# First sequence's k, q and v loaded in runs of six tokens and turned head by head, with the ranks of the first parts drawn anew

## The chip, the cores and the metric

The kernel runs on one core of a Trainium2 chip. The metric is the time of one execution on the device in microseconds (us), and the number given for a kernel is the median of several runs. PE is the engine of matrix products, DVE the vector engine, ACT the scalar engine, POOL and SP two more; SP's queue issues nearly all transfers. Each engine takes its instructions strictly in the order in which the program has them.

## What is computed

The inputs are q, k, v (8 sequences, 8 heads, 576 tokens, 64 numbers each), 32 packed queries p per head, two mixing vectors and three weight matrices. The weights come as 64-bit floats.

```python
def sm_attn(qq, kk, vv):                       # per head
    s = scale * qq @ kk.T;  a = softmax(s);  return a @ vv
x  = sm_attn(q, pp, pp)  with  pp = sm_attn(p, k, v)      # heads side by side: 8 x 576 x 512
xk = mu_k * x + (1 - mu_k) * x_prev;  xr = mu_r * x + (1 - mu_r) * x_prev   # x_prev: the token before
out = sigmoid(xr @ w_r) * (relu(xk @ w_k) ** 2 @ w_v)
```

## The kernel before

The 4608 tokens are worked off in nine blocks of 512. Every block needs products with w_r (the gates), w_k (the keys) and w_v (the values), and each of these is done three times in a reduced format with a high and a low part (`wr_h`, `wr_l`, `xh`, `xl`), so that one chunk of one tile is a triple of products 128x512. These triples are most of PE's work. The attention of a sequence is squeezed between them.

A planner inside the program (`Flow`) sets the order of everything. Each piece of work is a generator that says which engine it wants for how long by the planner's own estimate; the planner takes the piece that can start first, and ranks (the numbers `FIRST`, `RANK_...`, `RANK_LATE...`) break ties. The order is written into the program when it is built and nothing of it is decided on the chip. While the first sequence is under way, the planner puts products of the identity with itself into a spare bank (`fill`, L1809) wherever it believes PE to be idle. They are instructions like others: PE carries them out whether it has time or not.

The first sequence has a path of its own, in two halves h of four heads (two pairs each):

- `first_pair` loads a pair of heads of k or q into a tile `raw` of 96 partitions: token 96 c + p lies on partition p, so every piece moved is one token of one head, 256 bytes. There is one transfer per head.
- `transposed_on_pe` (k) and `first_transposed` (q, in two halves) turn a pair with six products per pair in transpose mode, 128 columns wide (L467, L498), and DVE and ACT copy the result from PSUM into `kT` and `qT`.
- `first_side(h)` is the chain: scores of p with k (`s1`, L560), the maximum (L793), the exponential (L800), the turning of the weights (L814, L815), their copy `aT` (L831 on ACT for h = 0, L826 on DVE for h = 1), the sum over v (`pv`, L581), the scaled result `pm` and its turning (`pT`, L602), the scores of q (`s2`, L615), a softmax over 32 columns (L628 to L641), the turning back (L648), its copies `a2t` (L653, L655), and the mixed inputs by products with the shares (`mixed_on_pe`, L969), whose high part ACT writes (L980) and whose low part DVE writes (L982).
- `first_gates` then does the gates of block 0 (L1128 to L1130). It begins when chunk 0 of half 0 is there and needs chunks 2 and 3 from half 1.
- `convert` splits a piece of a weight matrix into its two parts: three steps on ACT (L334, L336, L348) and two on DVE (L339, L350), from the transfer `st` on. There are 4 pieces of w_r, 8 of w_k and 8 of w_v.

Eight semaphores serve the transfers of SP and ACT in turn, so that a transfer waits for the one eight places before it. PSUM has two double banks `pa` for the large results of attention and single banks `m`.

Of the kernel before, what the change touches and what calls it, by code (L numbers as in the profile page):

```python
# [182 lines left out]
def attn_pack_channel_mix(ctx: ExitStack, tc: tile.TileContext, q, k, v, p, mu_k, mu_r, w_k, w_v, w_r, out):  # L183
# [4 lines left out]
    P = 128  # L188
# [17 lines left out]
    FIRST = 12.453, 12.081, 16.585, 10.332  # L206
    RANK_1, RANK_MIX, RANK_KEYS, RANK_R, RANK_W, RANK_W2, RANK_V, LOADS_1, RANK_SQ, RANK_REST, HOLD_V, HOLD_S = 14.383, 2.279, 9.364, 21.382, 11.434, 11.544, 16.223, 19.391, 0.152, -6.533, 0.05, 0.25
    RANK_LATE1 = -1.021
    RANK_LATE2 = 7.09
    RANK_LATE3 = 9.434  # L210
    RANK_LATE4 = 10.248
    RANK_LATE5 = 2.56
    RANK_LATE6 = 9.599
    RANK_LATE7 = 3.494
    RANK_LATE8 = 20.327
    RANK_LATE9 = 10.578
    RANK_LATE10 = 7.095
    RANK_LATE11 = 3.446
    RANK_LATE13 = 29.829
    RANK_LATE14 = 4.595  # L220
    RANK_LATE12 = 8.964
# [64 lines left out]
    for tag, n, size in (  # L286
        ("xk", NC, 2 * TB), ("sq", NF, 2 * TB), ("tmp", 4, WP), ("sig", 4, DM), ("kq", 4, S), 
        ("raw", 3, S), ("a2", 1, S), ("ex", 7, TB), ("e", 2, S), ("aT", 1, 5 * P), ("vt", 2, NPR * 5 * D),
# [3 lines left out]
    for j, size in enumerate((S, 5 * P)):  # L292
        sb.tile([P, size], F32, name="a", tag=f"a{j}")
# [94 lines left out]
    def loads(b):  # L388
        flow.spawn(packed(b), lrank(b) - 0.03)
        for src, tag in ((k, "kT"), (v, "vt"), (q, "qT")):  # L390
# [5 lines left out]
            for pr in range(NPR):  # L396
# [3 lines left out]
                if b < EARLY:  # L400

                    raw = tile_([P, 6, 2 * D], F32, space, slot, "raw")
                    for hh in range(2):
                        yield from load(
                            raw[:T6, :, hh * D:(hh + 1) * D], src[b, 2 * pr + hh].rearrange("(c p) d -> p c d", p=T6),
                            0.51, 0.6,
                        )
                        back_to_issue()
                    flow.spawn(transposed_on_pe(tag, b, pr, space, slot, raw), rank(b), flow.free["dma"] + LANDS)
                    continue  # L410

# [14 lines left out]
    def values_of(b, h):  # L426
# [4 lines left out]
        if b < MOVED:  # L431
# [25 lines left out]
    def transposed_on_pe(tag, b, pr, raw_space, raw_slot, raw):  # L457
# [6 lines left out]
        yield pe(0.66)  # L464
# [1373 lines left out]
```

## Time and profile before

| what | us |
|---|---|
| median of 3 runs (575.17 to 576.54) | 575.51 |
| the profiled execution's own time | 575.83 |
| its span in the trace | 574.0 |
| PE busy in the span (98%) | 564.7 |
| first product of the gates begins at | 31.94 |
| first product of the keys of block 0 begins at | 52.76 |

The span runs from the first instruction to the last; 1.83 us of the profiled execution lie outside it. A product's row in the trace is longer than the time after which the next one starts (390 ns on average against starts 0.23 us apart for the 128x512 products), so that the starts, not the durations, show the pace. One product of ordinary 32-bit numbers leaves two rows in the trace, one in transpose mode or in the reduced format leaves one. A filler leaves two.

### The profile page before, as it was taken

The numbers are of one execution on the slowest core, as the hardware profiler recorded it, in microseconds if no ns is written. First come the engines' busy times: TensorE is split into PE (matmuls) and PEld (weight loads), VectorE is DVE, ScalarE is ACT, GpSimd is POOL, SyncE is SP. The second block draws the span as 40 slices with busy tenths as digits, with TensorE's granted clock in tenths as the row PEclk, the third lists the DMA queues.
The fourth block names the chain that finished last, engine by engine and source line by source line (L and its number), as shares of the span: only waits on it lengthen the run. The fifth ranks groups of instructions, "written<-read, shape, count | busy, mean of one in ns | idle before, by whom it ended". The sixth has DMA issues, their size and how long they took to land.

```text
span 574.0 us, 9929 instructions
## 1 busy us (share of the span) xinstructions
PE 564.7 (98%) x3702; PEld 443.4 (77%) x3702; DVE 426.5 (74%) x792; ACT 342.0 (60%) x607; POOL 7.3 (1%) x36
## 2 busy tenths in 40 slices
PE   8999999999999999999999999999999999999996
PEld 7867767787677777777868777877788888888885
DVE  3797799928698778656982798078676799687974
ACT  2689979436376594374743585357545767645910
POOL 4000000000000000000000000000000000000000
PEclk9999999999999999999999999999999999999999
DMA  9898766664674660863466373200010010000025
GB/s 215 267 265 252 172 153 126 158 124 100 121 180 85 120 145 3 207 132 71 104 139 139 48 147 107 71 1 0 16 59 1 1 74 0 1 0 2 0 51 97
DMA packets 188000, 56.76 MB, mean 99 GB/s; under 512 B 165288, under 2 KB 180144, under 8 KB 187952
## 3 DMA queue, kind: packets, MB, share of 16 engines
q1 hardware_dynamic: 183536, 55.21, 41.8%
q10 hardware_dynamic: 4160, 0.66, 0.6%
q8 instruction: 29, 0.48, 0.4%
q0 software_dynamic: 256, 0.26, 0.2%
q14 instruction: 19, 0.16, 0.1%
HBM read 43.13 MB, written 12.98 MB: 98 GB/s over the span
## 4 chain that ended last, share of the span: by engine, by line
PE 78%; DVE 9%; ACT 6%; DMA 4%; SPq 2%; issue 1%; POOL 0%; ACTq 0%; DVEq 0%; POOLq 0%
PE ph L1083 8%; PE ph L1084 8%; PE ph L1085 8%; PE pvo L1179 7%; PE ph L1363 7%; PE pvo L1180 7%; PE pvo L1181 6%; PE ph L1640 6%; PE pr L1150 4%; PE pr L1151 4%; PE pr L1152 4%; DVE x L1050 3%; DMA st<-in_moe_w_r 2%; PE pa L923 2%; SPq L242 2%
## 5 line engine op out<-in xcount | busy, mean ns | idle before, releaser
L1179 PE MATMUL pvo<-wv_h,sq 128*128 128x512 f32 x224 | 89.3, 399 | 0.8 <-ACT r L1095 0.8
L1083 PE MATMUL ph<-xk,wk_h 128*128 128x512 f32 x224 | 89.5, 399 | 0.0
L1084 PE MATMUL ph<-xk,wk_h 128*128 128x512 f32 x224 | 87.4, 390 | 0.0
L1180 PE MATMUL pvo<-wv_l,sq 128*128 128x512 f32 x224 | 87.4, 390 | 0.0
L1085 PE MATMUL ph<-xk,wk_l 128*128 128x512 f32 x224 | 87.3, 390 | 0.0
L1181 PE MATMUL pvo<-wv_h,sq 128*128 128x512 f32 x224 | 87.3, 390 | 0.0
L1095 ACT ACTIVATE r<-ph 128x512 f32<-128x512 f32 x56 | 33.4, 597 | 60.6 <-PE ph L1085 55.6
L1050 DVE SCALAR_TENSOR_TENSOR x<-xt,mus,x 128x64 f32<-128x64 f32 (+7 forms) x117 | 52.8, 493 | 4.7 <-ACT x L1046 4.4
L1179 PEld LDWEIGHTS pvo<-wv_h,sq 128*128 128x128 f32 x224 | 42.1, 188 | 16.2 <-issue 6.3
L1046 ACT ACTIVATE x<-xt,mus 128x64 f32<-128x64 f32 (+7 forms) x117 | 53.8, 513 | 1.2 <-DVE sq L1104 0.9
L1102 DVE CAST sq<-r 128x512 fp32r<-128x512 f32 x56 | 23.3, 418 | 41.5 <-ACT r L1098 40.3
L1083 PEld LDWEIGHTS ph<-xk,wk_h 128*128 128x128 f32 x224 | 42.0, 188 | 13.1 <-issue 4.1
L1085 PEld LDWEIGHTS ph<-xk,wk_l 128*128 128x128 f32 x224 | 42.1, 188 | 9.0
L1181 PEld LDWEIGHTS pvo<-wv_h,sq 128*128 128x128 f32 x224 | 42.1, 188 | 8.9
L1180 PEld LDWEIGHTS pvo<-wv_l,sq 128*128 128x128 f32 x224 | 42.1, 188 | 8.1
L1084 PEld LDWEIGHTS ph<-xk,wk_h 128*128 128x128 f32 x224 | 42.1, 188 | 8.0
L946 ACT COPY xt<-pa 128x576 f32<-128x576 f32 x28 | 33.4, 1254 | 14.0 <-PE pa L923 13.8
L1104 DVE TENSOR_TENSOR sq<-r,sq 128x512 fp32r<-128x512 f32 x56 | 38.0, 681 | 1.0
L1161 ACT ACTIVATE sig<-pr 128x512 f32<-128x512 f32 x36 | 21.1, 599 | 29.1 <-PE pr L1152 22.7
L1150 PE MATMUL pr<-wr_h,xr 128*128 128x512 f32 x96 | 38.1, 397 | 0.0
L1151 PE MATMUL pr<-wr_l,xr 128*128 128x512 f32 x96 | 37.5, 390 | 0.0
L1152 PE MATMUL pr<-wr_h,xr 128*128 128x512 f32 x96 | 37.5, 390 | 0.0
(241 smaller groups left out, 1030.9 us busy)
## 6 DMA issues: line engine op xcount, KB each, us to landing
raw<-in_k SPq DMA_DIRECT2D x112, 72.0 KB, 2.8
raw<-in_q SPq DMA_DIRECT2D x112, 72.0 KB, 2.9
out<-sig SPq DMA_DIRECT2D x28, 256.0 KB, 2.5
st<-in_moe_w_k SPq DMA_DIRECT2D x8, 512.0 KB, 5.9
st<-in_moe_w_v SPq DMA_DIRECT2D x8, 512.0 KB, 5.9
vt<-in_v SPq DMA_DIRECT2D x24, 160.0 KB, 3.5
away<-blocks SPq DMA_DIRECT2D x12, 288.0 KB, 2.6
vt<-in_v SPq DMA_DIRECT2D x24, 128.0 KB, 3.8
```

What stands on the lines that cost most here:

```text
L1046: nc.scalar.mul(x32[:, o:o + n], xts[b, c][:, 1 + s:1 + s + n], mus[:, j, c:c + 1])
L1050: nc.vector.scalar_tensor_tensor(x32[:, o:o + n], xts[b, c][:, s:s + n], mus[:, j + 1, c:c + 1], x32[:, o:o + n], op0=ALU.mult, op1=ALU.add,)
L1083: nc.tensor.matmul(ph, wk_h[:, c, fs], xh, start=(c == 0), stop=False)
L1084: nc.tensor.matmul(ph, wk_h[:, c, fs], xl, start=False, stop=False)
L1085: nc.tensor.matmul(ph, wk_l[:, c, fs], xh, start=False, stop=(c == NC - 1))
L1150: nc.tensor.matmul(pr, xh[:, ts_], wr_h[:, c, :], start=(c == 0), stop=False)
L1151: nc.tensor.matmul(pr, xh[:, ts_], wr_l[:, c, :], start=False, stop=False)
L1152: nc.tensor.matmul(pr, xl[:, ts_], wr_h[:, c, :], start=False, stop=(c == NC - 1))
L1179: nc.tensor.matmul(pv[t], sh, wv_h[:, f, :], start=(n == 0), stop=False)
L1180: nc.tensor.matmul(pv[t], sh, wv_l[:, f, :], start=False, stop=False)
L1181: nc.tensor.matmul(pv[t], sl, wv_h[:, f, :], start=False, stop=(n == NF - 1))
L1363: nc.tensor.matmul(bank[2], w[:, fs], x, start=(not more and step == k == 0), stop=(step == 2 and k == 1), skip_group_check=True,)
```

## The change

For the first sequence only, a pair of heads of k or q is now one transfer. Six neighbouring tokens of a head lie on one partition, so that each piece moved is 1536 bytes. The two heads lie behind each other in `raw`, not side by side, so each head is turned by itself: twelve products with the identity per pair instead of six transposes, each 64 columns wide, alternately into the two halves of the PSUM bank, as ordinary products and not in transpose mode. The tokens come out in the order c, p with token 6 p + c; the maximum and sums don't mind, the weights are turned in six contiguous slices of 96 (six products instead of five), v is loaded in the same runs of six (three heads in the tile `vt`, the fourth in a tile `ex`; two transfers as before), and the order is undone when `a2t` is written. The copy `aT` becomes one instruction of 768 columns, `kT` of the first sequence is copied whole on ACT, `a2t` is copied by DVE and ACT together, and `s2` of half 1 now waits until half 0 has been turned back.

`first_gates` has another order: the gates start when the high part of chunk 0 exists; the two products with `xh` of three tiles come before those with `xl`, and the fourth tile's chunks 0 and 1 come before chunk 2. Line 1651 cuts the very last result of the program into two equal parts instead of three quarters and one quarter. All ranks have other values; they show only in the order below.

```diff
-        raw = tile_([P, 6, 2 * D], F32, space, slot, "raw")
-        for hh in range(2):
-            yield from load(
-                raw[:T6, :, hh * D:(hh + 1) * D], src[0, 2 * j + hh].rearrange("(c p) d -> p c d", p=T6), 0.51, 0.6,
-            )
-            back_to_issue()
+        raw = tile_([P, 2, 6, D], F32, space, slot, "raw")
+        yield from load(
+            raw[:T6].rearrange("p h c d -> p h (c d)"),
+            src[0, 2 * j:2 * j + 2].rearrange("h (p c) d -> p h (c d)", p=T6), 0.46, 0.85,
+        )
+        back_to_issue()
...
+        if not b:
+            vt = vt.rearrange("p a b -> p (a b)")[:T6, :3 * 6 * D].rearrange("p (a b) -> p a b", a=3)
+            more = sb.tile([P, 1, TB], F32, name="vt", tag=f"ex{h}")[:T6, :, :6 * D]
+            for x, n, heads in ((vt, 3, slice(h * NPR, h * NPR + 3)), (more, 1, slice(h * NPR + 3, (h + 1) * NPR))):
+                yield from load(x, v[0, heads].rearrange("h (p c) d -> p h (c d)", p=T6), 0.46, 0.36 * n)
...
-                nc.tensor.transpose(pT[:, hf, c * T6:(c + 1) * T6], raw[:T6, 3 * hf + c], ident[:T6, :T6])
+                for hh, half in enumerate(HALVES):
+                    nc.tensor.matmul(pT[half, hf, c * T6:(c + 1) * T6], raw[:T6, hh, 3 * hf + c], ident[:T6, :T6], start=True, stop=True)
...
-        for c in range(5):
-            n = P if c < 4 else S - NQ
+        for c in range(6):
             for pr in range(NPR):
                 rows = slice(32 * pr, 32 * pr + 32)
                 nc.tensor.matmul(
-                    pv[rows], aT[:n, c, rows], vt[:n, pr, c * D:(c + 1) * D], start=(c == 0), stop=(c == 4),
+                    pv[rows], aT[:T6, c, rows], vt[pr][:, c * D:(c + 1) * D], start=(c == 0), stop=(c == 5),
                 )
...
+        if h:
+            yield from flow.wait(("turned", 0))
         slot = yield from flow.take("pa")
         yield pe(1.6)
...
+    FIRST_GATES = ((0, 1, range(0, 1)),), ((0, 1, range(1, 2)),), ((0, 1, range(2, 3)), (0, 0, range(3))), (
+        (1, 1, range(3)), (1, 0, range(3)), (0, 1, range(3, 4)), (0, 0, range(3, 4)), (1, 1, range(3, 4)), (1, 0, range(3, 4)),
+    )
...
-                    for part in (slice(0, 3 * P), slice(3 * P, TB)):
+                    for part in (slice(0, 2 * P), slice(2 * P, TB)):
```

On PE at the program's start, before (fillers `spare`, k turned into `pa`, q turned into `pq`, `s1` from `kT`):

```order
L1809 MATMUL spare<-ident 128x128 x10
L467 MATMUL pa<-ident,raw 128x96 x6
L1809 MATMUL spare<-ident 128x128 x3
L467 MATMUL pa<-ident,raw 128x96 x6
L1775 MATMUL pu<-ident,rows 128x8
L1809 MATMUL spare<-ident 128x128
L498 MATMUL pq<-ident,raw 128x96 x3
L560 MATMUL pa<-kT,pt 64x288 x4
```

And now:

```order
L1834 MATMUL spare<-ident 128x128 x8
L464 MATMUL pa<-ident,raw 64x96 x24
L496 MATMUL pq<-ident,raw 64x96 x18
L558 MATMUL pa<-kT,pt 64x288 x4
L496 MATMUL pq<-ident,raw 64x96 x6
```

Both pairs of k and three of four halves of q now stand ahead of the first scores, where it was one half of q; in all there are 43 fillers before the first product of the gates in the old order, and 37 in the new one.

On PE from the last turning of q to the gates, before (`pv`, `pT`, `s2` as `both,qT`, the turning back as `ident,e`, the mixed inputs as `a2t,mub`):

```order
L1809 MATMUL spare<-ident 128x128 x7
L581 MATMUL pv<-vt,aT 32x64 x20
L1809 MATMUL spare<-ident 128x128 x3
L602 MATMUL pT<-ident,pm 128x128
L1809 MATMUL spare<-ident 128x128 x2
L615 MATMUL pa<-both,qT 128x64 x10
L648 MATMUL pa<-ident,e 112x128 x4
L648 MATMUL pa<-ident,e 128x128
L1809 MATMUL spare<-ident 128x128 x4
L969 MATMUL pa<-a2t,mub 128x512 x4
L1809 MATMUL spare<-ident 128x128 x9
L1128 MATMUL pr<-wr_h,xr 128x512
```

And now:

```order
L578 MATMUL pv<-vt,aT 32x64 x24
L496 MATMUL pq<-ident,raw 64x96 x6
L1834 MATMUL spare<-ident 128x128 x5
L599 MATMUL pT<-ident,pm 128x128
L1834 MATMUL spare<-ident 128x128 x15
L648 MATMUL pa<-ident,e 128x128 x4
L648 MATMUL pa<-ident,e 128x64
L614 MATMUL pa<-both,qT 128x64 x10
L981 MATMUL pa<-a2t,mub 128x512 x4
L1834 MATMUL spare<-ident 128x128 x4
L1156 MATMUL pr<-wr_h,xr 128x512
L1157 MATMUL pr<-wr_l,xr 128x512
```

The scores of q of half 1 have gone from before the turning back of half 0 to behind it.

On ACT around the copy `aT` of half 0, before:

```order
L475 COPY kT<-pa 128x288 x2
L800 ACTIVATE a,sm<-pa,nmx 128x576
L475 COPY kT<-pa 128x288
L831 COPY aT<-pa 128x512
L833 COPY aT<-pa 64x128
```

And now:

```order
L476 COPY kT<-pa 128x576 x2
L804 ACTIVATE a,sm<-pa,nmx 128x576
L476 COPY kT<-pa 128x576 x2
L334 ACTIVATE st<-st 128x512
L836 COPY aT<-pa 96x768
L336 ACTIVATE m<-st 128x512
```

The first step of the first piece of w_r (L334), which waits for a transfer, now stands in front of `aT`; it stood behind the exponential of `s2` (L633) before. On SP the four transfers of w_r are issued in front of half 1 of v, where they were behind it.

## Rows read from the trace of the kernel before

**Rows 1.** The page: the span, PE's busy time, and ACT's busy tenths in 40 equal slices of the span.

```profile
span 574.0 us, 9929 instructions
PE 564.7 (98%) x3702; PEld 443.4 (77%) x3702; DVE 426.5 (74%) x792; ACT 342.0 (60%) x607; POOL 7.3 (1%) x36
...
ACT  2689979436376594374743585357545767645910
```

**Rows 2.** PE in order of time in the front and at the first gates: start, length of the merged rows, line, product, count, idle time before and what ended it.

```profile
16.70 2.44 PE L615 MATMUL pa<-both,qT 128*128 128x64 f32 x20
...
20.11 1.73 PE L1809 MATMUL spare<-ident 128*128 128x128 f32 x14
21.76 0.90 PE L581 MATMUL pv<-vt,aT 128*32 128x64 f32 x40
...
26.50 0.67 PE L648 MATMUL pa<-ident,e 112*128 112x112 f32 x5
...
27.99 1.99 PE L969 MATMUL pa<-a2t,mub 64*128 64x512 f32 x8
29.91 2.27 PE L1809 MATMUL spare<-ident 128*128 128x128 f32 x18
31.94 0.47 PE L1128 MATMUL pr<-wr_h,xr 128*128 128x512 f32 x1
...
41.42 0.40 PE L1130 MATMUL pr<-wr_h,xr 128*128 128x512 f32 x1
42.32 1.99 PE L969 MATMUL pa<-a2t,mub 64*128 64x512 f32 x8 [0.51 <-DVE xr L982]
```

**Rows 3.** PE from 0 to 32 us, grouped by line: the fillers, with count, busy us, mean ns, idle time before.

```profile
L1809 PE MATMUL spare<-ident 128*128 128x128 f32 x86 | 14.0, 316 | 1.6 <-POOL ident masks.py:199 1.6
```

**Rows 4.** Stretches of PE on the chain of waits, in the front and (the last two) in sequence 2's attention: start, time until the next piece, what.

```profile
1.59 4.64 PE spare L1809 x20
...
8.95 1.12 PE pa L560 x8
10.07 0.65 PE pq L498 x6
...
125.98 1.30 PE pa L742 x80
...
129.68 1.13 PE pa L876 x32
```

**Rows 5.** ACT in order of time around the copy of aT and the first piece of w_r, and the issue of the w_r transfers on SP.

```profile
11.43 0.74 ACT L800 ACTIVATE a<-pa,nmx 128x576 f32<-128x576 f32 x1 [2.37 <-PE pa L467]
...
13.21 0.58 ACT L831 COPY aT<-pa 128x512 f32<-128x512 f32 x1 [0.66 <-PE pa L815]
13.69 0.26 ACT L833 COPY aT<-pa 64x128 f32<-64x128 f32 x1
...
14.49 2.23 SPq L242 DMA_DIRECT2D st<-in_moe_w_r  x4
...
21.98 0.69 ACT L334 ACTIVATE st<-st 128x512 uint32<-128x512 uint32 x1 [0.34 <-DMA st<-in_moe_w_r]
```

**Rows 6.** The page's list of transfers: the pieces of w_k, KB each, median us from issue to landing.

```profile
st<-in_moe_w_k SPq DMA_DIRECT2D x8, 512.0 KB, 5.9
```

**Rows 7.** A stretch of one us in the loading of the first sequence, and one in that of w_r: busy us of PE, PEld, DVE, ACT, POOL, the granted clock of PE, the busy share of the 16 transfer engines, GB/s.

```profile
9.00:10.00 1.00, 1.00 (x8) 0.36 (x9) 0.45 (x1) 0.05 (x1) 0.00 (x0) 1.00 1.13 255
...
21.00:22.00 1.00, 1.00 (x24) 0.88 (x26) 1.00 (x4) 0.66 (x2) 0.00 (x0) 1.00 1.04 426
```

**Rows 8.** DVE in order of time: the softmax of s2 of half 0, its first and its last instruction and one of the weights' steps in it.

```profile
19.19 0.82 DVE L628 TENSOR_REDUCE m<-pa 128x20 f32<-128x640 f32 x1 [1.60 <-PE pa L615]
...
23.25 0.70 DVE L339 SCALAR_TENSOR_TENSOR m<-m,st 128x512 uint32<-128x512 uint32 x1
...
23.87 0.82 DVE L641 TENSOR_TENSOR e<-e,m 128x640 f32<-128x640 f32 x1
```

**Rows 9.** PE in order of time at the two places behind the gates where its pace breaks by ACT: the turning of sequence 1's weights among the keys, and the first values.

```profile
60.01 0.39 PE L1085 MATMUL ph<-xk,wk_l 128*128 128x512 f32 x1
60.67 0.75 PE L814 MATMUL pa<-ident,a 128*128 128x128 f32 x4 [0.27 <-ACT a L800]
...
62.53 0.40 PE L1085 MATMUL ph<-xk,wk_l 128*128 128x512 f32 x1
63.01 0.75 PE L814 MATMUL pa<-ident,a 128*128 128x128 f32 x4
...
80.92 0.39 PE L1181 MATMUL pvo<-wv_h,sq 128*128 128x512 f32 x1
81.91 0.50 PE L1179 MATMUL pvo<-wv_h,sq 128*128 128x512 f32 x1 [0.60 <-ACT r L1095]
...
82.48 0.40 PE L1181 MATMUL pvo<-wv_h,sq 128*128 128x512 f32 x1
83.06 0.50 PE L1179 MATMUL pvo<-wv_h,sq 128*128 128x512 f32 x1 [0.18 <-ACT r L1095]
```

**Rows 10.** The end of the program in order of time: the two copies of the last result.

```profile
570.05 0.48 ACT L1719 COPY turn<-ph 128x384 f32<-128x384 f32 x1 [17.08 <-DMA out<-turn]
570.10 0.29 DVE L1722 COPY turn<-ph 128x128 f32<-128x128 f32 x1 [0.55 <-PE ph L1715]
```

More of the change, by code (lines that the diff above doesn't have):

```diff
@@ L645, in first_side @@
         e = e.rearrange("p (k a) b -> p k (a b)", a=NPR)
-        for k, (at, rows) in enumerate(CHUNKS):
-            bank, col = (0, at) if k < 4 else (1, 0)
-            nc.tensor.transpose(back_[:, bank, col:col + rows], e[:rows, k], ident[:rows, :rows])
+        for k, (_, rows) in enumerate(CHUNKS):
+            bank, col = divmod(k * P, 3 * P)
+            n = rows.stop - rows.start
+            nc.tensor.transpose(back_[:, bank, col:col + n], e[rows, k], ident[rows, rows])
         flow.give("xk", se)
+        flow.set(("turned", h))
         a2 = firsts["a2"][1][:, h]
-        last = CHUNKS[4][0]
-        yield act(last)
-        nc.scalar.copy(a2[:, 1:1 + last], back_[:, 0, :last])
-        yield act(S - last, after=0.0)
-        nc.scalar.copy(a2[:, 1 + last:], back_[:, 1, :S - last])
+        a2 = a2[:, 1:].rearrange("p (t c) -> p t c", c=6)
+        turned = flow.t
+        yield vec(4 * T6)
+        nc.vector.tensor_copy(a2[:, :, :4], back_[:, 0, :4 * T6].rearrange("p (c t) -> p t c", t=T6))
+        one = flow.t
+        yield act(4 * T6, after=turned)
+        nc.scalar.copy(a2[:, :, 4:], back_[:, 1, :2 * T6].rearrange("p (c t) -> p t c", t=T6))
+        flow.now.t = max(flow.t, one)
         flow.give("pa", slot)
@@ L812, in weights_of @@
         tp = banks(slot).rearrange("p a b -> p (a b)")
-        for c in range(4):
-            nc.tensor.transpose(tp[:, c * P:(c + 1) * P], a[:, c:NQ:4], ident)
-        nc.tensor.transpose(tp[:S - NQ, NQ:NQ + P], a[:, NQ:], ident)
+        pieces = [slice(c * T6, (c + 1) * T6) for c in range(6)]
+        if b:
+            pieces = [slice(c, NQ, 4) for c in range(4)] + [slice(NQ, S)]
+        for c, piece in enumerate(pieces):
+            n = T6 if not b else P if c < 4 else S - NQ
+            nc.tensor.transpose(tp[:n, c * P:(c + 1) * P], a[:, piece], ident)
         if h:
-            sT, aT = sa, tile_([P, 5, P], F32, "a", 1, "aT")
+            sT, aT = sa, tile_([P, 6, P], F32, "a", 1, "aT")
         else:
@@ L980, in mixed_on_pe @@
             nc.scalar.copy(xh, x)
+            res[0, 2 * h + c] = sx, xh, xl
+            flow.set((tag + " high", 0, 2 * h + c))
             yield vec(TB)
@@ new lines, in first_gates @@
+        yield from flow.wait(*(("qT", 0, j, hf) for j in range(NPR) for hf in range(2)), ("xr high", 0, 0))
+        opened, tiles = [], [slice(t * P, (t + 1) * P) for t in range(NT)]
+        for t in range(NT):
+            if t == NT - 1:
+                flow.keep_busy = 0.0
+                flow.give("m", 3)
+            slot = yield from flow.take("m")
+            opened.append((slot, ps.tile([P, DM], F32, name="pr", tag=f"m{slot}")))
+            for part in FIRST_GATES[t]:
+                yield from first_gate(opened, tiles, *part)
@@ new lines, in first_gate @@
+    def first_gate(opened, tiles, c, high, ts_of):
+        yield from flow.wait(("xr high" if high else "xr", 0, c), ("wr", c, 0))
+        _, xh, xl = xrs[0, c]
+        for t in ts_of:
+            pr, own = opened[t][1], tiles[t]
+            yield pe(0.455 if high else 0.228)
+            flow.now.t -= flow.LAG
+            if high:
+                nc.tensor.matmul(pr, xh[:, own], wr_h[:, c, :], start=(c == 0), stop=False)
+                nc.tensor.matmul(pr, xh[:, own], wr_l[:, c, :], start=False, stop=False)
+            else:
+                nc.tensor.matmul(pr, xl[:, own], wr_h[:, c, :], start=False, stop=(c == NC - 1))
```

121 lines of the change are left out of this document (52 added, 69 removed).

## The prediction

> **What bounds the kernel now.** I read the page first: PE is busy for 564.7 of 574.0 us [rows 1]. PE takes its work in order and is never empty, so the end moves only if the useful work starts at another time or loses less time behind its start. I therefore read PE in order of time, and took the first product of the gates, at 31.94 us [rows 2], as the border. Behind it lie the nine blocks, which the change leaves alone. Ahead of it lies the front: the first sequence's attention and the fillers.
>
> Is the front set by a chain of waits or by PE's own queue? Adding up the queue answers that. The twenty rows of the first fillers take 4.64 us from 1.59 on, 0.232 each [rows 4]; the other 66 of the 86 filler rows [rows 3] take (21.76 - 20.11)/14 = 0.118 each [rows 2], together 7.8. Turning k and q is 48 transposes at 0.65/6 = 0.11, 5.2 us; twice s1 is 2.24 [rows 4]; twice pv about 1.7, twice s2 about 4.7, the turning back 0.5, the mixed inputs 1.92 (27.99 to 29.91) [rows 2]; the rest (the weights, two small turnings, the shares) about 1.6. From 1.59 on that is 4.64 + 7.8 + 5.2 + 2.24 + 1.7 + 4.7 + 0.5 + 1.92 + 1.6 = 30.3, and 31.9 is reached, against 31.94 measured. So the fillers are not slack that can be eaten: they stand in the queue, and the new front can't be shorter than the sum of the new queue.
>
> Behind the border I looked for breaks in the pace of one product each 0.23 us. There are some: 0.67 us before the mixed inputs of half 1 (41.42 to 42.32) [rows 2], and four waits for ACT of 0.43, 0.25, 0.76 and 0.35 us, 1.8 in all [rows 9]. ACT is the neighbour that feeds PE there: its slices of 14 us are at 2, 6, 8, 9 and 9 tenths [rows 1]; its first step on a weight begins only at 21.98, when the transfer issued at 14.49 has landed [rows 5].
>
> **The change part by part.** First the queue of PE ahead of the border.
>
> Turning a pair of heads is now 12 ordinary products, and an ordinary product leaves two rows (L560: four products, eight rows), so 24 rows of 96 columns, two at a time in the two halves of the array. No row shows this shape; three stretches with their own shapes scale to it. L560, also two at a time, 288 columns: 1.12/8 x 96/288 = 0.047 per row. L876, eight at a time: 1.13/32 x 96/288 x 8/2 = 0.047. L742, four at a time, 64 columns: 1.30/80 x 96/64 x 4/2 = 0.049 [rows 4]. I take 0.047, 1.13 us per pair, 9.0 for eight pairs. Bounds: the products alone can't be quicker than some 0.040 if one sixth of those stretches is the change of shape (7.7 in all); if loading the turned matrix sets the pace, s2 shows 2.44/20 = 0.122 for 128 columns [rows 2], so 0.061 for 64 (11.7 in all). Against 5.2 this is +3.8, from +2.5 to +6.5.
>
> The Trainium skill, TensorEngine Tiling (Array Packing), Key Properties, says that a change of tiling mode drains TensorE, which speaks against this change: turning was in the shape of the fillers, now it isn't, in about six stretches. The trace of before has such changes only inside the stretches that I scaled, so their share is in the 0.047 once per stretch; by the page each of the six would cost its drain again, and by an estimate of 0.2 us from that sixth the sum would be 1.2 us longer, inside the bound above.
>
> Fillers: 37 instead of 43. The first ten become eight, four rows of 0.232 fewer (-0.93), and of the others 58 rows are left of 66 (-0.94): -1.9. pv has 24 instead of 20 products per half: 16 more rows at 0.90/40, +0.35. Two more turnings of weights at 0.12: +0.2. The first pair is turned while PE still has the pace of the first fillers, twice 0.118: +0.25. Sum of the queue: 3.8 - 1.9 + 0.35 + 0.2 + 0.25 = **+2.7**, and the border would be 34.6.
>
> What waits inside the new front? I followed the order with the durations above. The fillers end at 1.59 + 16 x 0.232 = 5.3; two pairs of k and three halves of q now stand ahead of s1, which ends near 10.3 (before 10.07 [rows 4]). Its exponential ends near 12.5 and frees the bank that the fourth pair of k needs; only behind that pair come the weights, at about 14.3, where ACT's copy aT began at 13.21 before [rows 5]. On ACT the first step of w_r (L334) now stands ahead of aT and waits for its transfer; queued behind it are aT, thus pv, pm and s2, so all of half 0. The transfer is the eleventh on SP instead of the twenty-first, and the tenth, the last pair of q, waits until PE has read the first pair of k. I put its issue at 8 to 9; with 5.9 [rows 6] to 7.5 us to landing (14.49 to 21.98 [rows 5]) it lands between 14 and 16.5. I take 15, some 0.5 us behind the moment when ACT would be free for it; the bounds are nothing and 2 us. From s2 to the end of the softmax DVE took 5.5 us, 19.19 to 24.69 [rows 8]; now four steps on weights and shares of about 0.65 stand in it where two stood, +1.3, but the scores of half 1 no longer stand between it and the turning back, which waited until 26.50 [rows 2]. So half 0 gets to the turning back at about 29, at the same time as PE's queue, and I add 0.3 for what doesn't fit. **Border 34.9, +3.0**, from +1.5 to +6.
>
> Then the gates. Eight triples stand ahead of half 1's mixed inputs instead of six, and the first product needs only ACT's high part. That covers the chain of half 1 better: of the breaks up to 52.76, which I count at about 1.7 us (20.8 us, less 16 triples of 0.68 and some 8.2 for the other products there), I take back **-0.5**, from 0 to -1.
>
> Then the waits for ACT of 1.8 us [rows 9]. ACT gets w_r 7 us sooner (15 instead of 21.98) and PE asks 2.5 us later, so ACT has several us more for the same steps. I take back **-1.5**, from 0 (the causes can lie in DVE or in a transfer) to -3 with smaller ones that no row names.
>
> Edits costed at nothing: fewer transfers on SP (eight fewer to issue) and the whole copies of kT are hidden by PE's queue, as above; if that cover went, a whole copy costs ACT some 0.3 us per pair on the chain of s1, twice. v comes in the same two transfers and is there before aT. The last result in halves: ACT's 0.48 for 384 columns gets shorter, DVE's 0.29 for 128 longer [rows 10], and the end moves by 0.1 either way; I count -0.1.
>
> Sum: 3.0 - 0.5 - 1.5 - 0.1 = **+0.9**. On the profiled execution's 575.83 that is 576.7; it stands 0.32 above the median of the three runs, 575.51, so the forecast of the median is **576.4**.
>
> **The rivals.** *Slower: the head of ACT's queue.* L334 ahead of aT holds half 0 until w_r is there. It decides from a landing of about 14.5 on; each us later is a us on the border, since nothing else can start. With a landing at 16.5 (+1.5) and the turning at its upper price (+2.7) the border is at 39.1, and the time is 575.5 + 7.2 - 0.5 - 1.5 - 0.1 = 580.6; the nearer form, landing at 16 and 0.053 per row (+1.0 and +1.15), gives 578.5. For it speaks that w_r's transfers took 7.5 us behind their issue and that PE's queue has no slack; against it, that the loads ahead of them have fewer pieces.
>
> *Faster: the loads.* In the loading of the first sequence the transfer engines are full at 255 GB/s, with whole rows of w_r they move 426 [rows 7]. If pieces of 1536 bytes go near the second figure, 3.5 MB and the first piece of w_r are there five us sooner; L334 never waits, ACT and DVE work through w_r and w_k in the front where they were idle, and the losses behind the border go, the 1.8 and small ones of later blocks, say 5 us in all. With a border of +2.5 the time is 575.5 + 2.5 - 0.5 - 5 = 572.5. The Trainium skill, DMA: Bandwidth & Descriptors, Specifications, points this way: it asks for at least 512 bytes per piece for line rate, and the old pieces have 256. The rows of the two rates agree in direction. Against this rival speaks that an earlier load can't shorten PE's queue.
>
> *No change in the front's length.* That the six-token runs do nothing at all (loads limited by the eight semaphores) leaves the queue's +2.7 and the -0.5 without the gain at ACT: 577.7, which lies with the slower cases.
>
> **How the numbers follow.** A measurement of this kernel can tell 0.3% from no change, 1.7 us. The forecast, front longer by about 3 and most of it given back, has 0.47: its own range is 574.6 to 577.2, all within 0.3%. The slower cases (queue dearer, L334 late, nothing given back) have 0.32, at 577.5 to 581. The faster one has 0.21, at 572 to 573.7. The range of 8 in 10 leaves out the ends of both: 573.2 to 579.5. So faster 0.21, same 0.47, slower 0.32.
>
> **What would show it.** In the trace of the changed kernel: the first product of the gates near 34.9 (right between 33.5 and 36); 24 rows of turning in about 1.1 us; L334 in front of aT with a wait for w_r of less than 1 us, and the first w_r step near 15; the waits at the keys and the first values gone or smaller. The forecast is wrong if the border lies before 33 or behind 37, if the keys of block 0 don't start within 3 us of 55.3 (52.76 + 3.0 - 0.5), or if the time comes or goes behind 100 us, where I count on nothing.

## The result, and the profile after

The changed kernel takes 581.62 us (median of 4 runs, 580.34 to 582.91), the kernel before 575.73 beside it (575.17 to 576.54): the ratio is 1.0101, 95% interval 1.0083 to 1.012. The forecast was 576.4, its range 573.2 to 579.5. The profiled execution is the slowest of the four, 582.91; its span is 580.9, 6.9 longer than before [rows 1].

The page of the changed kernel: span, busy time, and in 40 slices PE's busy tenths and granted clock.

```profile
span 580.9 us, 10185 instructions
...
PE 569.9 (98%) x3848; PEld 448.1 (77%) x3848; DVE 424.6 (73%) x789; ACT 340.7 (59%) x604; POOL 7.3 (1%) x36
...
PE   8799999999999999999999999999999999999997
...
PEclk9799999999999999999999999999999999999999
```

PE is still busy for 98%, so the page alone says little, but the second slice (14.5 to 29 us) has a 7 for PE and for its clock, where the kernel before has no such place. PE in order of time in the front and up to the keys, as in [rows 2] and [rows 4]:

```profile
5.31 2.28 PE L464 MATMUL pa<-ident,raw 96*64 96x96 f32 x48
7.42 1.94 PE L496 MATMUL pq<-ident,raw 96*64 96x96 f32 x36
...
10.91 1.21 PE L464 MATMUL pa<-ident,raw 96*64 96x96 f32 x24
12.05 0.71 PE L1834 MATMUL spare<-ident 128*128 128x128 f32 x4
...
14.85 1.19 PE L558 MATMUL pa<-kT,pt 128*64 128x288 f32 x8
19.59 1.51 PE L578 MATMUL pv<-vt,aT 96*32 96x64 f32 x48 [3.55 <-ACT aT L836]
21.03 2.19 PE L496 MATMUL pq<-ident,raw 96*64 96x96 f32 x24
...
28.04 0.72 PE L496 MATMUL pq<-ident,raw 96*64 96x96 f32 x12
28.68 0.88 PE L578 MATMUL pv<-vt,aT 96*32 96x64 f32 x48
...
40.75 0.47 PE L1156 MATMUL pr<-wr_h,xr 128*128 128x512 f32 x1
...
52.58 1.99 PE L981 MATMUL pa<-a2t,mub 64*128 64x512 f32 x8 [0.64 <-DVE xr L996]
...
55.73 0.66 PE L1011 MATMUL pa<-a2t,pm 64*128 64x65 f32 x8 [0.49 <-DVE xk L996]
...
62.57 0.50 PE L1096 MATMUL ph<-xk,wk_h 128*128 128x512 f32 x1
```

The reader is to see three things. A pair is turned in 1.14 us (10.91 to 12.05), as forecast. Then PE waits 3.55 us for the copy aT. And behind the wait the same shapes take longer: pv 1.51 us for half 0, 0.88 for half 1; 24 rows of turning 2.19 us, 1.21 earlier. The border, the first product of the gates, is at 40.75 instead of 31.94 (forecast 34.9), the first key at 62.57 instead of 52.76.

ACT in order of time, and the issue of w_r on SP, as in [rows 5]:

```profile
8.91 3.14 SPq L242 DMA_DIRECT2D st<-in_moe_w_r  x4
...
14.01 0.64 ACT L476 COPY kT<-pa 128x576 f32<-128x576 f32 x1 [0.98 <-PE pa L464]
18.20 0.65 ACT L334 ACTIVATE st<-st 128x512 uint32<-128x512 uint32 x1 [3.56 <-DMA st<-in_moe_w_r]
18.76 0.78 ACT L836 COPY aT<-pa 96x768 f32<-96x768 f32 x1
```

L334 stands ahead of aT in ACT's queue and waits 3.56 us for w_r; aT, which needs nothing of w_r, waits with it. Windows, with the columns of [rows 7] (the last three: granted clock, share of the transfer engines, GB/s):

```profile
2.00:6.00 4.00, 4.00 (x30) 3.77 (x31) 0.00 (x0) 0.22 (x2) 3.89 (x11) 1.00 0.99 278
6.00:10.00 4.00, 3.93 (x84) 3.44 (x80) 1.75 (x5) 1.28 (x2) 0.69 (x3) 1.00 0.98 218
10.00:14.00 4.00, 4.00 (x71) 3.41 (x68) 1.91 (x9) 1.36 (x3) 0.00 (x0) 1.00 1.06 283
14.00:18.00 4.00, 2.04 (x16) 1.21 (x15) 0.76 (x1) 0.64 (x1) 0.00 (x0) 1.00 1.05 321
...
19.00:20.00 1.00, 0.41 (x16) 0.41 (x20) 0.00 (x0) 1.00 (x2) 0.00 (x0) 0.58 1.04 428
20.00:25.00 5.00, 5.00 (x77) 4.57 (x67) 2.21 (x5) 3.39 (x10) 0.00 (x0) 0.50 1.09 273
25.00:26.00 1.00, 1.00 (x7) 0.98 (x6) 0.14 (x1) 1.00 (x3) 0.00 (x0) 0.51 0.96 341
26.00:30.00 4.00, 4.00 (x91) 3.72 (x90) 3.27 (x7) 2.23 (x5) 0.00 (x0) 1.00 0.64 118
```

From 19.2 to 26 the granted clock is at its lower level (0.50, that is 1.2 of 2.4 GHz): PE works in 6.4 of these us, and does 3.2 us of work. And the transfers run at 218 to 283 GB/s while k, q and v come in pieces of 1536 bytes, at full share. Over the whole stretch from 2 to 14 us that is little more than before. One window of the kernel before, then the same of the changed one:

```profile
2.00:14.00 12.00, 11.82 (x86) 10.56 (x85) 4.67 (x14) 2.88 (x9) 4.55 (x13) 1.00 1.05 247
```

```profile
2.00:14.00 12.00, 11.93 (x175) 10.62 (x175) 3.65 (x13) 2.86 (x7) 4.58 (x13) 1.00 1.01 260
```

### The profile page after: what moved, and what is told of

It is laid out like the page before. It is cut to its first block, busy times and chain, and to the rows that moved or that the text cites. A ratio compares the mean times of both kernels' runs of the same rounds, so it can differ in the third digit from the quotient of the medians.

```text
span 580.9 us, 10185 instructions
## 1 busy us (share of the span) xinstructions
PE 569.9 (98%) x3848; PEld 448.1 (77%) x3848; DVE 424.6 (73%) x789; ACT 340.7 (59%) x604; POOL 7.3 (1%) x36
## 4 chain that ended last, share of the span: by engine, by line
PE 90%; DVE 5%; DMA 2%; ACT 1%; issue 1%; POOL 0%; SPq 0%; DVEq 0%; POOLq 0%
PE ph L1096 9%; PE ph L1097 9%; PE ph L1098 9%; PE pvo L1204 8%; PE pvo L1205 8%; PE pvo L1206 8%; PE ph L1388 7%; PE ph L1665 7%; PE pr L1175 4%; PE pr L1176 4%; PE pr L1177 4%; PE pa L935 2%; PE spare L1834 2%; DMA st<-in_moe_w_r 2%; PE pa L746 2%; PE pa L724 1%
## 5 line engine op out<-in xcount | busy, mean ns | idle before, releaser
L1115 DVE CAST sq<-r 128x512 fp32r<-128x512 f32 x56 | 23.5, 420 | 57.2 <-ACT r L1111 55.7
```

## The experiments

First theory, W: half 0 is held by w_r at the head of ACT's queue, and the half clock follows from PE's idle time. Its rival, Q: PE's queue with the dearer turning sets the front. Every run names what it was to tell apart. Border and keys are those of each run's one profiled execution, times are medians, and each ratio is to the kernel before, run beside it.

| run | waits of PE ahead of the border, us | granted clock 0.50, about | border | keys | time | ratio (95%) |
|---|---|---|---|---|---|---|
| before | none over 0.2 | never | 31.94 | 52.76 | 575.73 | |
| after | aT 3.55 | 19.2 to 26 | 40.75 | 62.57 | 581.62 | 1.0101 (1.0083-1.0120) |
| e1_swap | q 0.85, scores of half 1 1.76 | 21.5 to 31.8 | 41.30 | 63.17 | 582.22 | 1.0116 (1.0090-1.0143) |
| e2_behind | v 1.40 | 24.7 to 31.5 | 40.05 | 61.95 | 581.36 | 1.0097 (1.0082-1.0111) |
| e3_fill | none | 51.9 to 55.3 | 38.70 | 62.17 | 582.34 | 1.0117 (1.0104-1.0130) |
| e4_turn | none | never | 36.77 | 57.59 | 580.18 | 1.0083 (1.0070-1.0096) |
| e5_whole | k 0.91, q 1.28 and 0.58, aT 0.43, v 1.13 | 9.5 to 19.8, and 53.9 to 57.3 | 39.83 | 63.95 | 583.74 | 1.0139 (1.0125-1.0153) |
| e7_cover | q 0.43, softmax of half 0 1.14 | 32.6 to 39.4 | 39.35 | 61.13 | 581.78 | 1.0107 (1.0094-1.0121) |
| e8_vheld | aT of half 1 2.02 | 22.4 to 29.3 | 39.33 | 62.05 | 583.35 | 1.0135 (1.0121-1.0149) |
| e10_wholeheld | k 2.09, five others of 0.41 to 0.56 | 8.1 to 18.4 | 39.47 | 62.41 | 583.54 | 1.0149 (1.0135-1.0163) |
| e11_cover2 | pv of half 1 0.52 and 0.16 | never | 36.61 | 58.97 | 580.18 | 1.0093 (1.0080-1.0107) |
| e12_nofill | aT of half 1 1.25 | never | 31.52 | 52.35 | 575.59 | 1.0003 (0.9994-1.0012) |

Borders of single executions differ by up to 1 us for a reason that no edit sets. The first fillers have a slow pace, and the first turning keeps it for a shorter or a longer time. Below are its 48 rows in the changed kernel and in e3, then turning under the lower clock in the changed kernel (shortest, median and longest duration in ns, first and last start):

```profile
L464 PE MATMUL pa<-ident,raw x48: 246/246/376, 5.3 to 7.3; 96*64 96x96 f32 x48
```

```profile
L464 PE MATMUL pa<-ident,raw x48: 246/367/422, 5.3 to 8.3; 96*64 96x96 f32 x48
```

```profile
L496 PE MATMUL pq<-ident,raw x24: 367/367/422, 21.0 to 22.8; 96*64 96x96 f32 x24
```

The slow rows of e3 last 367 ns, as long as those at a granted clock of 0.50, although the windows show 1.00 there. e2 and e15 lose 1.0 to 1.1 us by it too, e16 0.4.

**e1_swap** moves one step, **e2_behind** four:

```diff
+held_back(first, L334)      # e1: first L334 issued right behind the copy aT of half 0
+held_back(first, L334, L336, L339)  # e2: steps on two pieces of w_r, behind ACT's copy of the turned pm of half 0
```

> The changed kernel, with one step moved on ACT: the first step on w_r (L334 there), which stood ahead of the copy aT of half 0 and waited 3.56 us for its transfer, is issued right behind aT; the other steps on w_r keep their places ahead of the exponential of half 1. Theory T (half 0 is held at the head of ACT's queue by w_r's late transfer, PE stands idle and falls to half its clock): aT starts near 14.7 instead of 18.76 and pv near 15.5 instead of 19.59; the exponential of half 1 still waits for w_r, to about 20.6, so PE stands idle for about 2 us at another place; first product of the gates near 36.5 instead of 40.75, time near 577.6. Rival R (PE's queue, with the dearer turning, sets the front): the border stays near 40 and the time at 581.6, since no work of PE is taken away.

> The changed kernel, with all ACT and DVE steps on the first two pieces of w_r held until behind the shares of half 0 (the step that adds its two exponentials' sums), so that nothing of half 0 stands behind the transfer of w_r in any queue. Theory T: no idle time of PE over 1 us ahead of the border, granted clock 1.00 throughout the front, border at 34.6 to 35.5 (the queue's +2.7), time 575.7 to 577. Rival R (the turning and the queue are dearer than thought): border at 38 or later, time at 580 or more.

Both moved the wait, and neither the median. In e1, ACT's exponential of half 1 now stands behind the steps on w_r. In e2, pv of half 0 starts at 17.0, no step of half 0 waits, and still PE stands and its clock falls, now for v of half 1. One row of PE and two windows of e2:

```profile
24.60 1.87 PE L591 MATMUL pv<-vt,aT 96*32 96x64 f32 x48 [1.40 <-DMA vt<-in_v]
```

```profile
20.00:24.00 4.00, 3.20 (x36) 2.94 (x34) 2.83 (x5) 3.82 (x9) 0.00 (x0) 1.00 1.09 279
...
25.00:31.00 6.00, 6.00 (x71) 5.61 (x71) 4.24 (x10) 3.55 (x8) 0.00 (x0) 0.50 0.74 162
```

So W in its simple form, that the step on w_r ahead of aT is the whole cause, falls. The medians mix executions, though: of e1's six, the one with a mean granted clock of 1.000 took 579.17, the three at 0.991 took 583.54 to 584.68.

**e3_fill** keeps the wait and fills it:

```diff
+if not h: 15 x fill()       # ahead of pv of half 0
```

> The changed kernel with fifteen more fillers (30 rows, about 3.5 us) put ahead of pv of half 0, where PE stood idle for 3.55 us behind the copy aT; the wait itself stays. If the fall of the granted clock to 0.50 between 20 and 26 us cost about 3 us of the border, as theory T has it, the clock stays at 1.00, the border comes to about 37.8 and the time to about 578.6. If the clock cost nothing (the work at half pace lay beside other waits), border 40.7 and 581.6; if the fillers run past the landing of aT, up to 1 us more.

The clock stayed up and the border came 2.05 us sooner, although 3.55 us of fillers (16.95 to 20.50) lie where PE was idle: the half clock does cost the border some 3 us. But the keys came at 62.17, 0.4 us sooner only: DVE now made PE wait 0.56 and 0.85 us for xr at 50 and 51.5, and the clock fell there.

```profile
50.21 0.49 PE L1162 MATMUL pr<-wr_h,xr 128*128 128x512 f32 x1 [0.56 <-DVE xr L999]
51.55 1.77 PE L984 MATMUL pa<-a2t,mub 64*128 64x512 f32 x4 [0.85 <-DVE xr L999]
```

**e4_turn** is the turning alone, in the kernel before:

```diff
-nc.tensor.transpose(pT[...], raw[:T6, 3 * hf + c], ident[:T6, :T6])
+for hh, half in enumerate(HALVES):
+    nc.tensor.matmul(pT[half, ...], raw[:T6, 3 * hf + c, half], ident[:T6, :T6])
```

> The kernel before, with k and q of the first sequence turned head by head by products with the identity (two of 64 columns in the place of one transpose), all loads, ranks and orders as before. It prices the turning alone: 24 pairs-of-three (eight whole pairs) at 1.06 to 1.14 us instead of 0.65 us. If PE's queue sets the front, the border goes from 31.94 to about 35.2 and the time, with some of it given back as in the changed kernel, to 577 to 579. If the turning lies beside other waits, the border moves by less than 1 us and the time stays at 575.7.

The border moved by 4.83, the time by 4.7, with no wait and no half clock. Turning all eight pairs takes 9.24 us, each group from its start to the next row's, where the 48 transposes took 4.64: +4.60. One pair and the border:

```profile
8.44 1.21 PE L468 MATMUL pa<-ident,raw 96*64 96x96 f32 x24
9.58 0.22 PE L1777 MATMUL pu<-ident,rows 8*128 8x8 f32 x1
...
36.77 0.47 PE L1130 MATMUL pr<-wr_h,xr 128*128 128x512 f32 x1
```

**e5_whole** takes the turning out of the changed kernel; it needs two heads in a row, so k and q come in 256-byte pieces again:

```diff
-raw[:T6].rearrange("p h c d -> p h (c d)"), src[0, 2 * j:2 * j + 2].rearrange("h (p c) d -> p h (c d)", p=T6)
+raw[:T6, :, :D], src[0, 2 * j].rearrange("(p c) d -> p c d", p=T6)          # and D: from 2 * j + 1
-nc.tensor.matmul(pT[half, ...], raw[:T6, hh, 3 * hf + c], ident[:T6, :T6], ...)   # twice
+nc.tensor.transpose(pT[...], raw[:T6, 3 * hf + c], ident[:T6, :T6])
```

> The changed kernel, with its k and q pairs turned whole again (one transpose of 128 columns instead of two products of 64) and for that loaded into a row of two heads (pieces of 256 bytes in place of 1536, two transfers for a pair), in the same order on every engine. The turning takes 0.65 us per pair instead of 1.14, so PE's queue ahead of the border is 4.0 us shorter, and about 0.8 more if the changes of shape cost too. Theory Q (the queue sets the front, as the run with the turning alone in the kernel before says: +4.7 us): border near 36, keys near 57.8, time near 577. Theory W (in the changed kernel the front is set by the landing of w_r ahead of the copy aT, then by the half clock): L334 still ends its wait near 18.2, if the pieces of 1536 bytes were no faster, pv starts near 19.6, PE stands idle some 5 us instead of 3.55, and only the turning behind pv gets shorter: border 39 to 40, time 579.5 to 580.5.

Q falls, and of W only the border comes out, with other waits: PE has some 4.6 us less to do, and the border comes 0.9 sooner, the keys 1.4 later. PE waits for k and q at once, since the transfers start slower: 171 GB/s from 2 to 6 us in the window of e5 below, where the changed kernel has 278. The share is 0.79 here, so the engines were not full. The first two pairs of k and of q are issued head by head, the last head at 6.28, where the changed kernel issues the last two of their four transfers from 1.66 on. So the number of transfers is a rival to the size of the pieces, and no run here separates the two. A window and a row of e5, then a row of the changed kernel:

```profile
2.00:6.00 4.00, 4.00 (x22) 4.00 (x21) 0.00 (x0) 0.22 (x2) 3.89 (x11) 1.00 0.79 171
...
6.28 0.63 SPq L370 DMA_DIRECT2D raw<-in_q  x1
```

```profile
1.66 0.94 SPq L242 DMA_DIRECT2D raw<-in_q  x2
```

**e7_cover, e8_vheld, e10_wholeheld** keep e2's hold on w_r and take its wait for v away, by fillers moved (the number is the same), by v loaded ahead of w_r, and by that with whole pairs:

```diff
+if h: 7 x fill()            # e7: ahead of pv of half 1, seven fewer ahead of the turning back
-FIRST = 14.439, 10.225, 14.505, 15.686
+FIRST = 16.5, 16.6, 16.7, 16.8    # e8; e10 with the pairs of e5
```

> The kernel of e2_behind (no step on w_r ahead of half 0), with seven of the fifteen fillers that stand ahead of the first turning back put ahead of pv of half 1, where e2_behind waited 1.40 us for v and then ran at half clock to 31.5. The number of fillers is the same; only their place differs. If the clock's fall costs 3 us and nothing else holds the front, the border comes from 40.05 to 35.2 to 35.8, the keys from 61.95 to about 57.5, and the time to about 577. If DVE, which was busy almost without a break from 28 to 50 us in all kernels with keys at 62, sets the keys, the border may come sooner, but the keys stay behind 60 and the time at 580 or more, as in e3_fill.

> The kernel of e2_behind, with the loads of v ahead of those of w_r by their ranks (FIRST 16.5 to 16.8), as in the kernel before; the planner then puts seven fillers more ahead of the turning back, and seven fewer elsewhere, by itself. Theory W: v of half 1 is there when PE comes to it, w_r lands near 21, behind the head of nothing that half 0 needs; no wait of PE over 0.7 us, granted clock 1.00 throughout, border 35 to 36.5, time 576 to 578. If DVE's steps on w_r, which stand ahead of its copy aT of half 1, hold half 1, there is a wait there of 1 to 2 us, the clock falls, and the time is 579 to 582.

> e5_whole and e8_vheld together: pairs turned whole, v ahead of w_r, and no step on w_r ahead of half 0. What is left of the change is the order of the first gates, the copies of six chunks, the shares' order and the ranks. If the turning and the waits on w_r and v are what made the changed kernel slower, the border comes to 31 to 32.5 and the time to 572 to 574.5, below the kernel before, since the 2.6 us that the new ranks give back behind the keys stay. If the waits come back at another place, since PE's queue is shorter than the transfers, the border is at 34 to 36 and the time at 575 to 577.

Each met the next wait, as the table has it. e7 came out as its second case (keys behind 60, time over 580), e8 as its second in kind (a wait of 2.02 us, time 583.35), e10 as neither. In e7 it was the softmax of half 0 on DVE:

```profile
30.13 0.86 PE L666 MATMUL pa<-ident,e 128*128 128x128 f32 x5 [1.14 <-DVE e L658]
```

In e8, pv of half 1 (23.38) waited for DVE's copy aT, which stood behind a step on w_r, so it is again w_r at the head of a queue:

```profile
21.12 0.69 DVE L352 SCALAR_TENSOR_TENSOR m<-m,st 128x512 uint32<-128x512 uint32 x1 [3.78 <-ACT m L349]
...
22.33 0.95 DVE L848 COPY aT<-pa 96x768 f32<-96x768 f32 x1
```

**e11_cover2, e12_nofill, e9_oldranks, e14_laterranks**:

```diff
+if h: 7 x fill()            # e11: e7, with two fewer instead of seven fewer ahead of the turning back
-7 x fill()                  # e12: before, ahead of pv of half 1
-FIRST, RANK_*, HOLD_* of after    +those of before         # e9, in the changed kernel
-RANK_1, RANK_KEYS ... HOLD_S of before    +those of after  # e14, in the kernel before
```

> The kernel of e7_cover with five more fillers ahead of the first turning back (13 of the 15 of the changed kernel), where e7_cover waited 1.14 us for DVE and then ran at half clock to 39. Theory C: no wait over 0.7 us ahead of the border, granted clock 1.00 to there, border near 36.1 to 36.5 instead of 39.35 (34.2 for the queue, 0.98 for the second pair of k, and 1.2 of fillers more), keys near 58.0 to 58.5, time 577.5 to 579. If the front was held by DVE or by transfers, and the clock only followed, border and keys stay within 1 us of e7_cover's 39.35 and 61.13, and the time near 581.

> The kernel before, without the seven fillers (14 rows, 1.65 us) ahead of pv of half 1, where PE waits for DVE's copy aT until about 21.7 in any case. Nothing else differs. Theory C (each wait of about 1.1 us or more in the front is followed by some 6.4 us at half clock, and that costs about 3 us, in every kernel of this study): PE stands idle 1.5 us at 20.2 to 21.7, the granted clock is 0.50 from about 22 to 28, the border goes from 31.94 to 34.5 to 35, and the time to 577.5 to 578.5, though PE has less to do. If a wait costs only itself, border and time stay as they are.

> The changed kernel with all ranks and loads' ranks of the kernel before. The planner then puts v ahead of w_r, and L334 behind aT of half 0 but ahead of the exponential of half 1. Theory C: that exponential waits for w_r's transfer, to 21 or later, PE stands idle for over 1.1 us behind its second turning of scores, the clock falls for 6.4 us, border 39 to 41. Behind the keys the 2.6 us are not given back, since these come from the new ranks, so the time is 582 to 585. If the ranks anew were the cost of the change, the time is 578 to 580.

> The kernel before, with the ranks of the later parts and the two holds of the changed kernel (RANK_1, RANK_KEYS, RANK_R, RANK_W, RANK_W2, RANK_V, LOADS_1, RANK_SQ, RANK_REST, HOLD_V, HOLD_S); the loads and turnings of the first sequence, its mixing and the weights' first loads keep their ranks. If the 2.6 us that the changed kernel gains behind the keys come from the new ranks, the border stays at 32 to 32.5, blocks 0 to 2 get shorter by 1.2, 1.0 and 0.4 us, and the time is 572.5 to 573.5, below both kernels. If they come from the later border alone (weights further ahead of PE), the time stays at 575 to 576.5.

e11 is the one run that got the changed front free of long waits and of the half clock: border 36.61 and keys 58.97, a little behind what was expected, and its profiled execution, the fastest of five, took 579.41 (span 577.5) against 582.91, the slowest of four. By the medians the gain is smaller, 580.18 against 581.62, ratios 1.0093 and 1.0101, whose intervals overlap, so it is not shown. Its longest waits ahead of the border:

```profile
24.30 0.31 PE L594 MATMUL pv<-vt,aT 96*32 96x64 f32 x6 [0.52 <-DVE rs L601]
24.78 0.86 PE L594 MATMUL pv<-vt,aT 96*32 96x64 f32 x42 [0.16 <-DMA vt<-in_v]
```

e12 contradicts the rule that I had made of the waits (Theory C): PE stood 1.25 us, nothing followed, and the clock stayed at 1.00. Nor did it fall behind the wait of 1.13 us for v in e5. PE in e12 (pv and the border), and its clock behind the wait:

```profile
21.50 0.90 PE L581 MATMUL pv<-vt,aT 128*32 128x64 f32 x40 [1.25 <-DVE aT L826]
...
31.52 0.47 PE L1128 MATMUL pr<-wr_h,xr 128*128 128x512 f32 x1
```

```profile
22.00:26.00 4.00, 4.00 (x51) 3.69 (x40) 4.00 (x10) 3.84 (x9) 0.00 (x0) 1.00 0.89 264
```

e9 took 593.56 (1.0320, 1.0301 to 1.0339), far over what was expected, with waits of 3.15 and 5.21 us for ACT's exponential: the new code with the old ranks is 12 us worse than with its own, so in the new code the new ranks are no cost. e14 took 582.05 (1.0112, 1.0096 to 1.0129), missed: border 32.29, but keys 53.85, and from there the first two blocks are 1.3 and 4.9 us longer. The later ranks are no gain by themselves in the old code.

**e16_onepiece, e15_oldgates, e17_gates, e18_tail** price single terms:

```diff
-FIRST = 14.439, 10.225, 14.505, 15.686
+FIRST = 14.439, 16.6, 16.7, 16.8          # e16: three pieces of w_r behind v
-first_gate(...) by FIRST_GATES             # e15: after, with the loop of before; e17: the reverse, in before
-slice(0, 3 * P), slice(3 * P, TB)
+slice(0, 2 * P), slice(2 * P, TB)         # e18, in before
```

> The changed kernel, with the second to fourth piece of w_r loaded behind v of half 1 (FIRST 14.439, 16.6, 16.7, 16.8); the first piece keeps its place, and L334 still stands ahead of aT. If the three pieces behind it shared its transfer time, it now lands some 1.9 MB into the transfers instead of 2.5, at 15 to 16: L334's wait is 0 to 1.5 us instead of 3.56, v lands sooner too, no wait of PE over 1.5 us; the border is at 35 to 37.5 and the time at 577 to 580. If k, q and v ahead of it are what it waits for, L334 ends its wait at 17.5 or later, the clock falls, and border (40 to 41) and time (581 to 582) stay.

> The changed kernel with the first gates in the order of the kernel before (each triple whole, six triples ahead of half 1's turning back in place of eight with the low parts last). The front is as in the changed kernel (border 40.75, one filler pair more). If the new order made the stretch from border to keys longer, that stretch goes from 21.8 back to 20.8 and the time to 580.5; if it made it shorter, as the prediction had it (0.5 us), it goes to 22.3 or more and the time to 582 to 583.

> The kernel before with the first gates in the order of the changed kernel (high parts first, eight triples ahead of half 1's turning back), all else as before; the planner then needs five fillers fewer around the border (10 rows, about 1.2 us). As the prediction had it, the order gives 0.5 us or more: border at 30.8 to 31.5, keys at 51.2 to 52.3, time 574 to 575.2. As the changed kernel showed it (21.8 from border to keys instead of 20.8), the stretch gets longer by 0.6 to 1, and the time is 575.5 to 576.5.

> The kernel before with the last result copied in halves of 256 columns instead of 384 and 128, nothing else. Prediction: -0.1, so 575.4; at most 0.3 either way. The changed kernel's end behind its last product was 4.3 us instead of 4.6, which would be -0.3.

e16 took 584.83 (1.0156, 1.0133 to 1.0179): w_r's first piece, issued at 9.33 with v and not w_r behind it, landed at 19.19, not sooner, and PE waited 4.10 us. So w_r's own pieces behind it do not account for the delay. ACT in e16:

```profile
19.19 0.65 ACT L334 ACTIVATE st<-st 128x512 uint32<-128x512 uint32 x1 [4.11 <-DMA st<-in_moe_w_r]
```

e15 took 591.47 (1.0281, 1.0253 to 1.0309): keys 24.2 us behind the border instead of 21.8. Its front is the changed kernel's, but in its profile w_r landed at 17.29, PE waited 1.53 us, the clock stayed at 1.00, and the border came at 38.45 with 0.9 us of fillers more. Its keys came at 62.66, as the changed kernel's did (62.57). In its profile (590.60 against 582.91) the loss lies behind them: the first two blocks are 2.5 and 4.6 us longer than the changed kernel's.

```profile
18.68 0.88 PE L578 MATMUL pv<-vt,aT 96*32 96x64 f32 x48 [1.53 <-ACT aT L836]
```

e17 took 574.89 against 575.61 (0.9978, 0.9967 to 0.9990), the only run better than both kernels, by 1.3 us by the ratio. Where it gains is not shown: in its profile (575.46) border and keys come no sooner than before, 20.8 us apart as before, and it has five fillers fewer besides.

```profile
32.27 0.48 PE L1144 MATMUL pr<-wr_h,xr 128*128 128x512 f32 x1
...
53.10 0.50 PE L1084 MATMUL ph<-xk,wk_h 128*128 128x512 f32 x1 [0.47 <-ACT sig L1174]
```

e18 took 575.55 (1.0000, 0.9989 to 1.0010).

## Why the prediction was wrong

**PE's queue: the sum held, in part by luck.** Forecast 34.6 without waits. e3 has no idle row ahead of its border: 38.70, less 3.55 of added fillers, less 0.98 that its first turning lost at the slow pace (5.31 to 8.40, where the changed kernel shows 5.31 to 7.42), is 34.2. The expectation of e11 called that 0.98 a wait for k; the durations above say that it is pace. The price of 0.047 per row held (1.14/24 = 0.0475). But the old transposes were priced too high, 0.11 instead of 4.64/48 = 0.097, so the turning is +4.6 and not +3.8; all other terms came to -2.3 and not -1.1, so that the errors cancel. For one, the added rows of pv cost nothing (together 0.88 us long at 28.68, 0.90 before [rows 2]), where +0.35 was counted. And the +0.25 for the slow pace was 0 in the changed kernel's profile and about 1 in e3's.

The Trainium skill, TensorEngine Tiling (Array Packing), Key Properties, says that a change of tiling mode drains the engine. The prediction put up to 1.2 us more on it, by an estimate. In e4 the border moved by 4.83, and the turning's own rows account for 4.60, so at most 0.2 is left outside them. Inside them a cost per stretch is seen: 12 rows took 0.64 us (28.04 to 28.68), 24 took 1.14, 48 took 2.11, that is some 0.04 per row and 0.15 per stretch, by an estimate from these three. It is part of the 0.047; whether it is that drain, no run here shows.

**The step that failed: "I take 15", for the landing of w_r, and "I add 0.3 for what doesn't fit".** The issue was right (8 to 9; it was 8.91), the landing was 18.20, 9.3 us later, outside the bounds of 14 to 16.5. They came from the time of other transfers of the kernel before (5.9 and 7.5 us [rows 5, 6]), not from the bytes under way. By the windows the engines moved 16 us at 278, 218, 283 and 321 GB/s, 4.4 MB, by 18 us; k, q, half of v, the piece and the rows of mu are 1.18 + 1.18 + 0.59 + 0.52 + 0.26 = 3.7. So other pieces were moved beside it; which ones is open, since it landed no sooner in e16, with only v's pieces issued next behind it. The landing also differs between executions of the same front: 18.20, 17.29 (e15) and 18.78 (e3). L334's wait is 3.56 instead of less than 1. The fall of the clock, 3.2 us, had no term in the sum at all. In the profile: 34.2 + 3.55 + 3.2 = 40.95, against 40.75.

**But that wait is not the cause by itself.** Where it was taken away (e1, e2, e7, e8), other waits of 0.85 to 2.02 us came next, for q, for v, for the softmax on DVE, and twice behind steps on w_r at another place (e1 on ACT, e8 on DVE), and the keys stayed between 61.1 and 63.2. e11 is free of long waits, and its border is still 4.7 us later than before; 1.2 of that are the five fillers that it adds (ten rows), 0.7 its short waits, and the rest, 2.8, is near the queue's 2.3. And e4 shows that the turning alone costs 4.7 us in the old plan; in the changed kernel fewer fillers and the rest set 2.3 against it. The forecast let 2.0 of a longer front come back; in e4 0.6 did (keys +4.83, end +4.22).

**The second step that failed: gates, -0.5.** Border to keys is 21.8 us instead of 20.8 in the changed kernel, 22.4 in e11 and 23.5 in e3 (a fall of the clock included), so the term was +1.0 or more. DVE is late there: PE waits 0.64 and 0.49 us for it (52.58, 55.73) where [rows 2] have one wait of 0.51. What the order of the gates is worth by itself stays open. Alone it gave 1.3 us (e17), but not in the stretch that the term names, and undone in the changed kernel it cost 10 by the medians (e15), in the profile behind the keys.

**Waits for ACT, -1.5:** behind the keys 2.6 us came back by the last product (+9.8 at the keys, +7.2 there), more than forecast. What gives them is open: neither the later ranks alone (e14) nor a later border alone (e4) do.

**Tail, -0.1:** right (e18).

**The sum in the profile** (of the slowest execution)**:** queue +2.3, wait +3.55, half clock +3.2, less 0.2 that the rows overlap: border +8.8; gates +1.0; back behind the keys -2.6; end -0.3: +6.9.

**The rivals.** The head of ACT's queue was the mechanism of this profile; its price stopped at a landing of 16.5, with a time of 580.6. The faster loads fell: from 2 to 14 us the engines moved 260 GB/s against 247 before, 5% more, both at full share, and w_r's rows reached 428 again. The Trainium skill, DMA: Bandwidth & Descriptors, Specifications, asks for at least 512 bytes for line rate. Over that whole stretch this case shows only 5% between pieces of 256 and of 1536 bytes. What the change did give is the start, 278 against 171 GB/s from 2 to 6 us (e5), by longer pieces or by fewer transfers.

**Open.** The half clock is not the whole loss. The changed kernel itself took 580.34 in the execution with a mean granted clock of 0.999, and 582.91 in the one at 0.992; the first is still 4.6 us over the kernel before. Other executions at 1.000 took 579.17 (e1), 581.27 (e3), 583.46 (e8) and 583.54 (e10), and there are no traces of them. A kernel without DVE's late chain was not tried, nor one with whole pairs and a start as fast as the changed kernel's. So no run gives the 5.9 us back, and their split between queue, waits and clock is read from one profile.

## What to carry to other kernels

Bound a transfer's landing by the bytes that are under way with it, not by the duration of its like elsewhere, and let no step that waits for one stand ahead of work in the same queue that needs nothing of it. Where transfers, the softmax and PE end within two us of each other, taking one wait away shows the next: price the edit that lengthens PE's queue first, here the turning, since none of the reorderings tried gave that back. An edit that may gain (the gates' order, 1.3 us in e17) is worth trying alone in the old plan.

## What was not expected of the hardware

The granted clock fell to 0.50 for 6.8 us at or behind waits of 3.55, 1.40 and 1.14 us (after, e2, e7; in e7 2.4 us after the wait had ended), and did not behind 1.25 (e12) and 1.53 (e15): the length of one wait does not decide it. The pace at the program's start is that of 0.50 (367 ns for a row of turning in e3, as at 21 us in the changed kernel), while the windows show 1.00. A transfer of 0.5 MB took 7.4 to 9.9 us from issue to landing (7.4 in e15, 9.3 in after, 9.7 in e3, 9.9 in e16).
